# Scores' factors on another engine, with their operand in another memory, and a new plan, in a fused attention and two-MoE kernel

## The chip, the cores and the metric

One core of a Trainium2 chip runs the whole kernel. The metric is the device time in microseconds (us) of one execution. Engines, by the names that the profile uses: PE is TensorE (PEld its weight loads), DVE is VectorE, ACT is ScalarE, POOL is GpSimd, SP is SyncE, which issues the DMAs. Each engine takes its instructions in the order of the program.

## What is computed

A linear attention with decay, then two feed-forward layers on its output, all in float32 (the weights of both layers arrive as float64):

```python
# r, k, v: 4 x 8 x 768 x 48 (batch, head, time, channel); w, u: 8 x 48
for t in range(S):
    cur = einsum('bhd,bhe->bhde', u * k[t], v[t])
    y[t] = einsum('bhd,bhde->bhe', r[t], state + cur)
    state = w[..., None] * state + einsum('bhd,bhe->bhde', k[t], v[t])
x = y as 3072 x 384
h = maximum(maximum(x @ w1, x @ w2), x @ w3)   # 384 -> 768
x = h @ w_out                                  # 768 -> 384
g = x @ w_gate                                 # 384 -> 1536
out = (silu(g) * (x @ w_val)) @ w_out2         # 1536 -> 384
```

## The kernel before

Time is cut into six blocks of 128 steps (NB = 6), and with four batches (B = 4) this makes 24 units of attention; unit n is batch n % 4 of block n // 4. The products of the two layers take float32 in two halves: for each operand a high half and a low half, three matmuls for a product (`product`, lines 420 to 424).

**A unit** has these steps. `load_unit` (285) brings `qk` (112 x 1024, the transposed r and k) and `nat` (128 x 1152: k, v, r by time). `prep_scores` (302) multiplies each half of `qk` by powers of the decay `P`: the scores' factors. `prep_bonus` (306) makes two products for the bonus term, `prep_keys` (311) scales the keys by `PT`. `scores` (328) is 8 matmuls into two banks of PSUM; `bonus` sums rows (L318), `fill` writes a diagonal (L326, ScalarE), `select` (337) copies the masked scores over it (L338, two instructions). `apply` (344) makes y from the state (L355) and from the masked scores (L364). `evacuate` copies y out. `outer` (374) is 8 matmuls, the outer products of keys and values (L383); `decay` (388) scales the state and `update` (392) adds the outer products (L397), or copies them in block 0 (L395). Each pool of PSUM `ps_s` (tags s0, s1), `ps_y`, `ps_u` holds one bank a tag; `ps_m` has four banks in turn for everything else.

**A weight job** is a piece of 576 columns (384 for w_b) of float64 weights that VectorE and ScalarE turn into two halves: `scale` (ScalarE), `top` (L250, L252), `rest` (L258, L260), `power` (L265) on VectorE, `put_hi` and `to_float` on ScalarE, `put_lo` (L276) on GpSimd or VectorE. Jobs 0 to 11 make w_a (the first layer's three matrices, two jobs for each of its 6 tiles f), 12 to 17 w_b, the rest w_c. Three buffers hold raw weights.

**The stages.** After the set-up come the four units of block 0, then `branch` (589): all engines read a flag and skip a slow path (`recurrence`, not taken here). Block i of the first layer is then 18 products `m(i, f, j)` of 9 matmuls, with the units of block i + 1 between them, and the products `o`. After block 5 the second layer runs through its six blocks (g, silu, oo).

**What sets the order.** The code between lines 499 and 804 issues everything by hand. `order` (600 to 620) is TensorE's sequence, written out. For the other engines class `Plan` (88) keeps, for each step, the engines that may take it with a cost on each, what it needs, and a lag; `run` picks, again and again, the step that can start earliest by its own clock, weighted by what hangs on it, and emits it. So the costs in the table decide the order on VectorE, GpSimd, ScalarE and SyncE. In block 0 `scaled`, the factors, may go to VectorE or GpSimd (`both`), later to GpSimd alone (`one`). `warm` fills TensorE's planned idle time in block 0 with matmuls that nobody reads.

The lines that the change turns on:

```python
def prep_scores(n, q, eng):
    a = inp[n][0][:, q]
    eng.tensor_tensor(out=a, in0=a, in1=P[0:112], op=ALU.mult)
...
        p, tag = (ps_m, "m") if n < B else (ps_u, "u")
...
add(("scaled", n, q), both if first else one, [("load", n)],
```

Of the kernel before, what the change touches and what calls it, by code (L numbers as in the profile page):

```python
# [8 lines left out]
F32 = mybir.dt.float32  # L9
# [5 lines left out]
ALU = mybir.AluOpType  # L15
# [4 lines left out]
T = 128  # L20
# [7 lines left out]
FAR = 3  # L28
# [59 lines left out]
class Plan:  # L88
# [4 lines left out]
    def __init__(self, free, tensor_order):  # L93
        self.steps, self.free, self.tensor_order = {}, dict(free), tensor_order
        self.behind = {}

    def add(self, key, on, needs, do, lag=0.0, at=0.0, behind=None):


        if behind is not None:  # L100
            self.behind[key] = behind
        self.steps[key] = (on, list(needs), do, lag, at)

    def run(self, idle, hop=0.1):
# [22 lines left out]
        done, ready = {}, {}  # L127

# [8 lines left out]
        while ready:  # L137
# [28 lines left out]
def rwkv_moe(ctx: ExitStack, tc: tile.TileContext, qk, nat, kn, vn, rn, wcol, wh, uh, wup1, wout1, wup2, out):  # L166
# [332 lines left out]
    with tc.manual_schedule():  # L499
# [84 lines left out]
        def flag(_):  # L584
            nc.vector.tensor_reduce(out=off[:, NPAIR:], in_=spare[:, T:], axis=AX.X, op=ALU.max)
            nc.vector.tensor_scalar(out=slow_i, in0=off[:, NPAIR:], scalar1=1.0, scalar2=None, op0=ALU.min)
            nc.vector.tensor_copy(slow, slow_i)

        def branch(_):
            warm(8)  # L590
            general = nc.values_load(slow_i[0:1, 0:1], min_val=0, max_val=1)
            with tc.If(general != 0):
                recurrence(tc, kn, vn, rn, wh, uh, [xr[0]] + [x2[i] for i in range(1, FAR)] + y_far, h_tile)

# [49 lines left out]
        add = plan.add  # L644
        both, one = {"dve": 0.9, "pool": 1.4}, {"pool": 1.45}

# [7 lines left out]
        for k, (key, z, n, _) in enumerate(jobs):  # L654
            early = key[0] == "c" and key[1] < ASIDE
            own, pace, space = {}, [], []
            TOP, REST, POWER, share = (1.9, 1.8, 0.7, n / HALF) if key[0] != "c" else (2.2, 2.2, 0.9, 1.0) if early else (1.25, 1.25, 0.46, 1.0)
            if early:
# [6 lines left out]
            else:  # L665
# [8 lines left out]
            add(("float", k), cast, [("rest", k)], lambda e, k=k: to_float(k), **own)  # L674
            add(("lo", k), {"pool": 1.6 * share, "dve": 0.9 * share}, [("float", k), ("power", k), ("hi", k)],
                lambda e, k=k: put_lo(k, engine[e]), **own)
# [19 lines left out]
        for n in range(NB * B):  # L696
# [12 lines left out]
            add(("bonus", n), {"dve": 1.2, "pool": 2.15} if first else {"pool": 2.15}, [("arrived", n)],  # L709
                lambda e, n=n: prep_bonus(n, engine[e]))  # L710
            add(("keys", n), {"pool": 1.05}, [("bonus", n)], lambda e, n=n: prep_keys(n), at=9.6)
            pair = {2: 0, 4: 2}.get(n, n - 1 if n > 4 else None)
            add(("s", n), {"pe": 1.3}, [("scaled", n, 0), ("scaled", n, 1)] + bank_free["s", n]
                + ([("select", pair, 0), ("select", pair, 1)] if pair is not None else []), lambda e, n=n: scores(n))
            add(("a0", n), {"dve": 0.55}, [("bonus", n)] + ([("y", two)] if n > 1 else []), lambda e, n=n: bonus(n))
            for x in range(2):
# [6 lines left out]
                lambda e, n=n: evacuate(n))  # L723
            add(("u", n), {"pe": 0.02 if last else 0.6}, [("y", n), ("keys", n)] + bank_free["u", n]
                + ([("update", n - 1)] if n > B and n <= (NB - 1) * B else []), lambda e, n=n: outer(n))
            if first:
                add(("update", n), {"act": 0.55}, [("u", n)], lambda e, n=n: update(n))
            elif not last:
                add(("decay", n), {"pool": 0.62}, [("y", n)], lambda e, n=n: decay(n, engine[e]))
# [3 lines left out]
        add(("branch",), {"none": 0.0}, rows0 + [("flag",), ("u", B - 1)]  # L733
            + [("fill", n, x) for n in range(B) for x in range(2)], branch)
# [151 lines left out]
```

## Time and profile before

| | before |
|---|---|
| time, median of 3 runs | 882.13 us (881.97 to 882.39) |
| the profiled execution: its own time | 882.0 us |
| the profiled execution: its span | 880.3 us |
| TensorE busy | 855.5 us (97%) |
| VectorE busy | 437.9 us (50%) |
| ScalarE busy | 317.1 us (36%) |
| GpSimd busy | 242.4 us (28%) |
| chain that ended last | PE 87%, DVE 6%, issue 2% |

The span runs from the first to the last instruction of the profiled execution. The shares are means over the whole span, and the stages differ: VectorE is busy half of the time on average, but the page's slices show it at nine tenths in the first stages and at two tenths in the second layer. The granted clock of TensorE is a share of 2.4 GHz; it is at 0.5 in some stretches before 114 us and at 1.0 after that.

### The profile page before, as it was taken

What the parts mean: (1) busy time and instruction counts of PE and PEld (TensorE: products, weight loads), DVE (VectorE), ACT (ScalarE), POOL (GpSimd) and SP (SyncE); (2) the same over time, 40 slices, a digit from 0 to 9 for tenths busy, and PEclk for the clock granted to TensorE, in tenths of its full rate; (3) what the DMA queues carried; (4) which work ended last, traced back from release to release, by engine and by line L of the source; (5) the groups of instructions that cost most, each with busy time, mean ns of one, the idle gap of its engine ahead of it and who ended that gap; (6) DMA issues with size and microseconds to landing.
All of it is one profiled execution on the core that took longest, in us unless ns stands there. A gap on an engine that the chain in (4) does not pass through costs nothing.

```text
span 880.3 us, 11968 instructions
## 1 busy us (share of the span) xinstructions
PE 855.5 (97%) x4790; PEld 702.0 (80%) x4790; DVE 437.9 (50%) x610; ACT 317.1 (36%) x633; POOL 242.4 (28%) x207
## 2 busy tenths in 40 slices
PE   7888799999999999999999999999999999999998
PEld 6776588887887887888888888888888888888886
DVE  7899978765955954323469522222222222222212
ACT  4655654453453442222356421231122122123111
POOL 7386556454754753110123200010010000001000
PEclk9889999999999999999999999999999999999999
DMA  9545325534544543313034010000000000000001
GB/s 286 216 132 190 113 101 176 172 119 156 169 140 149 176 156 123 131 72 130 1 108 135 1 37 0 1 36 1 1 36 1 1 0 36 1 1 36 0 1 37
DMA packets 21723, 74.34 MB, mean 84 GB/s; under 512 B 2496, under 2 KB 3392, under 8 KB 20896
## 3 DMA queue, kind: packets, MB, share of 16 engines
q1 hardware_dynamic: 21664, 73.54, 25.2%
q8 instruction: 38, 0.62, 0.3%
q14 instruction: 21, 0.17, 0.1%
HBM read 58.39 MB, written 14.16 MB: 82 GB/s over the span
## 4 chain that ended last, share of the span: by engine, by line
PE 87%; DVE 6%; issue 2%; ACT 0%; DVEq 0%; ACTq 0%
PE g L423 11%; PE g L422 11%; PE g L424 11%; PE m L422 8%; PE m L424 7%; PE m L423 7%; PE oo L423 6%; PE oo L422 6%; PE oo L424 6%; PE o L422 3%; PE o L424 3%; PE o L423 3%; PE s L335 2%; PE y L364 2%; PE y L355 2%
## 5 line engine op out<-in xcount | busy, mean ns | idle before, releaser
L479 DVE TENSOR_TENSOR g<-mm,g 128x512 f32<-128x512 f32 x72 | 50.1, 696 | 242.1 <-PE g L424 242.1
L422 PE MATMUL g<-xhi,w_c 128*128 128x512 f32 x432 | 168.0, 389 | 0.0
L423 PE MATMUL g<-xlo,w_c 128*128 128x512 f32 x432 | 168.0, 389 | 0.0
L424 PE MATMUL g<-xhi,w_c 128*128 128x512 f32 x432 | 168.0, 389 | 0.0
L422 PE MATMUL m<-xhi,w_a 128*128 128x512 f32 x324 | 132.9, 410 | 1.1 <-DVE hs L456 1.1
L423 PE MATMUL m<-xlo,w_a 128*128 128x512 f32 x324 | 128.8, 398 | 1.9 <-POOL xlo L417 1.9
L424 PE MATMUL m<-xhi,w_a 128*128 128x512 f32 x324 | 128.3, 396 | 0.1
L417 POOL TENSOR_TENSOR xlo<-x,xhi 128x512 fp32r<-128x512 f32 x12 | 16.4, 1373 | 340.0 <-DVE g L479 281.8
L475 ACT ACTIVATE mm<-g 128x512 f32<-128x512 f32 x72 | 43.1, 599 | 152.5 <-PE g L424 152.4
L422 PEld LDWEIGHTS g<-xhi,w_c 128*128 128x128 f32 x432 | 81.1, 188 | 17.0
L424 PEld LDWEIGHTS g<-xhi,w_c 128*128 128x128 f32 x432 | 81.1, 188 | 16.8
L423 PEld LDWEIGHTS g<-xlo,w_c 128*128 128x128 f32 x432 | 81.1, 188 | 16.8
L484 ACT CAST gs<-g 128x512 fp32r<-128x512 f32 x72 | 42.3, 587 | 134.8 <-DVE g L479 134.8
L422 PE MATMUL oo<-gs,w_c 128*128 128x512 f32 x216 | 84.0, 389 | 0.0
L423 PE MATMUL oo<-gs,w_c 128*128 128x512 f32 x216 | 84.0, 389 | 0.0
L424 PE MATMUL oo<-gs,w_c 128*128 128x512 f32 x216 | 84.0, 389 | 0.0
L304 POOL TENSOR_TENSOR qk<-qk,P 112x512 f32<-112x512 f32 x45 | 67.2, 1499 | 41.4 <-DMA qk<-in_qk 41.4
L422 PEld LDWEIGHTS m<-xhi,w_a 128*128 128x128 f32 x324 | 62.2, 192 | 17.0 <-DVE hs L456 1.3
L424 PEld LDWEIGHTS m<-xhi,w_a 128*128 128x128 f32 x324 | 62.2, 192 | 14.2 <-POOL w_a L276 0.6
L423 PEld LDWEIGHTS m<-xlo,w_a 128*128 128x128 f32 x324 | 62.2, 192 | 14.1 <-POOL xlo L417 2.2
L456 DVE TENSOR_TENSOR gs<-g,gs 128x512 fp32r<-128x512 f32 x72 | 49.7, 690 | 40.9 <-ACT gs L484 40.9
L326 ACT ACTIVATE am<-aeye,a 128x128 f32<-128x128 f32 x192 | 59.2, 390 | 20.6 <-DVE a L318 20.6
(115 smaller groups left out, 1225.3 us busy)
## 6 DMA issues: line engine op xcount, KB each, us to landing
raw<-in_wup SPq DMA_DIRECT2D x36, 576.0 KB, 5.5
nat<-in_nat SPq DMA_DIRECT2D x22, 576.0 KB, 5.5
qk<-in_qk SPq DMA_DIRECT2D x24, 448.0 KB, 4.9
aside<-parts SPq DMA_DIRECT2D x12, 576.0 KB, 3.7
w_c<-aside SPq DMA_DIRECT2D x6, 1152.0 KB, 5.2
out<-ob SPq DMA_DIRECT2D x18, 256.0 KB, 2.1
y<-x SPq DMA_DIRECT2D x3, 768.0 KB, 10.7
raw<-in_wout SPq DMA_DIRECT2D x6, 384.0 KB, 4.5
```

The lines of the kernel that those rows point to most:

```text
L304: eng.tensor_tensor(out=a, in0=a, in1=P[0:112], op=ALU.mult)
L326: eng.mul(o, aeye, f)
L335: nc.tensor.matmul(sc[n][x][:, j], a[r:r + D, 1, j], a[r:r + D, 0, j], start=True, stop=True)
L355: nc.tensor.matmul(y[r:r + m, j], st[b][r:r + D, j * D:j * D + m], a[r:r + D, 0, j], start=j == 0, stop=False, skip_group_check=True)
L364: nc.tensor.matmul(y[r:r + m, j], v[:, h * D:h * D + m], am[:, x, j], start=not i, stop=True, skip_group_check=bool(i))
L422: nc.tensor.matmul(p, wh_, xh, start=first, stop=False)
L423: nc.tensor.matmul(p, wh_, xl, start=False, stop=False)
L424: nc.tensor.matmul(p, wl_, xh, start=False, stop=last)
L456: nc.vector.tensor_tensor(out=g[1], in0=p, in1=g[0].bitcast(F32), op=ALU.subtract)
L475: nc.scalar.activation(out=hs[i, f], in_=banks["g", i, f, 0], func=AF.Silu)
L479: nc.vector.tensor_tensor(out=p, in0=hs[i, f], in1=p, op=ALU.mult)
L484: nc.scalar.copy(t[:, 0], banks["g", i, f, 1])
```

## The change

Four things are changed. The new file is longer by 7 lines ahead of the helpers and by 29 at its end, so that L304 before is L311 after, L441 is L448 and L383 is L390.

1. From unit 4 on the factors (`scaled`) go to VectorE, and their second operand is a copy of `P` in PSUM (`late["P"]`, named `powers`), which ScalarE makes right after the branch in the bank of the pool `ps_u`.
2. That bank is no longer free for outer products, so from unit 4 on these are written into bank s0, where the unit's scores were. The scores of unit n + 1 therefore wait for the state update of unit n.
3. The outer products of block 0 leave the sequence ahead of the branch: those of units 0 and 1 come after `m(0, 0, 0)`, those of units 2 and 3 after `m(0, 1, 0)`. The slow path takes its scratch memory from elsewhere.
4. The plan has a port: steps on GpSimd, and the listed steps on VectorE (`SHARED`, without the factors from unit 4 on), start no earlier than the last of them ends. Its costs for these steps are lower than before.

```diff
+    SHARED = ("top", "rest", "power", "lo", "xlo", "ylo", "scaled", "bonus", "choose")
...
                     start, cost = max(t, free[e]), steps[k][0][e]
+                    if e == "pool" or e == "dve" and k[0] in self.SHARED and (k[0], k[1] > 3) != ("scaled", True):
+                        start = max(start, port)
...
             free[e] = start + cost
+            if e == "pool" or e == "dve" and k[0] in self.SHARED and (k[0], k[1] > 3) != ("scaled", True):
+                port = start + cost
...
-        eng.tensor_tensor(out=a, in0=a, in1=P[0:112], op=ALU.mult)
+        eng.tensor_tensor(out=a, in0=a, in1=late["P"] if n >= B else P[0:112], op=ALU.mult)
...
-            p, tag = (ps_m, "m") if n < B else (ps_u, "u")
+            p, tag = (ps_m, "m") if n < B else (ps_s, "s0")
...
+        def powers(_):
+            t = ps_u.tile([128, NPAIR, T], F32, tag="u", name="powers")
+            late["P"] = t[0:112]
+            nc.scalar.copy(late["P"], P[0:112])
...
-        order = [(q, n) for q, n in zip("ssyuyussyuyu", (0, 1, 0, 0, 1, 1, 2, 3, 2, 2, 3, 3))]
+        order = [(q, n) for q, n in zip("ssyyssyy", (0, 1, 0, 1, 2, 3, 2, 3))]
...
+                order += [("u", n) for n in range(B) if i == 0 and n // 2 == f]
...
-        both, one = {"dve": 0.9, "pool": 1.4}, {"pool": 1.45}
+        both, one = {"dve": 0.65, "pool": 1.07}, {"pool": 1.07}
...
-                add(("scaled", n, q), both if first else one, [("load", n)],
+                add(("scaled", n, q), both if first else {"dve": 0.69}, [("load", n)] + ([] if first else [("powers",)]),
...
-                + ([("select", pair, 0), ("select", pair, 1)] if pair is not None else []), lambda e, n=n: scores(n))
+                + ([("select", pair, 0), ("select", pair, 1)] if pair is not None else [])
+                + ([("update", n - 1)] if B < n <= (NB - 1) * B else []), lambda e, n=n: scores(n))
```

In the listings below, `a_0` to `a_3` are the row sums of the bonus of units 0 to 3, `am` a unit's masked scores, `r` and `kv` the r, k and v of units 2 and 3, `nat` those of the others, `t` and `raw` a weight job's tiles, `h` and `m` the products of the first layer.

VectorE ahead of the branch, where it prepares block 0; before:

```order
L318 TENSOR_REDUCE a_0_213<-nat_109 128x8
L304 TENSOR_TENSOR qk_113<-qk_113,P 112x512
L338 COPY_PREDICATED am_214<-mask,s_0_226 128x512
L338 COPY_PREDICATED am_214<-mask,s_0_227 128x512
L318 TENSOR_REDUCE a_1_260<-nat_114 128x8
L308 TENSOR_TENSOR r_106<-kv_118,r_106 128x384
L309 TENSOR_TENSOR r_106<-r_106,ub 128x384
L304 TENSOR_TENSOR qk_117<-qk_117,P 112x512
```

and after:

```order
L325 TENSOR_REDUCE a_0_227<-nat_109 128x8
L345 COPY_PREDICATED am_228<-mask,s_0_216 128x512
L345 COPY_PREDICATED am_228<-mask,s_0_217 128x512
L325 TENSOR_REDUCE a_1_267<-nat_114 128x8
L592 TENSOR_REDUCE off<-spare 128x1
L593 TENSOR_SCALAR slow_i<-off 128x1
L594 CAST slow<-slow_i 128x1
L345 COPY_PREDICATED am_268<-mask,s_1_249 128x512
L325 TENSOR_REDUCE a_2_302<-r_106 128x8
```

The bonus products of units 2 and 3 and the factors of units 1 and 2 have left VectorE's queue; both are on GpSimd now. VectorE keeps the factors of unit 0.

VectorE in block 0 behind the branch, at the second and third product of its first tile; before:

```order
L441 TENSOR_TENSOR m_0_2_725<-h_0_721,m_0_2_725 128x512
L265 TENSOR_SCALAR raw_676<-t_707 128x576
L250 TENSOR_SCALAR t_741<-t_741 128x576
L252 SCALAR_TENSOR_TENSOR t_741<-raw_704,t_741 128x576
L318 TENSOR_REDUCE a_4_806<-nat_670 128x8
L456 TENSOR_TENSOR hs_0_789<-m_0_2_725,hs_0_789 128x512
```

and after:

```order
L448 TENSOR_TENSOR m_0_2_695<-h_0_654,m_0_2_695 128x512
L311 TENSOR_TENSOR qk_668<-qk_668,powers 112x512 x2
L272 TENSOR_SCALAR raw_617<-t_642 128x576
L463 TENSOR_TENSOR hs_0_739<-m_0_2_695,hs_0_739 128x512
L325 TENSOR_REDUCE a_4_756<-nat_669 128x8
```

Unit 4's two factors stand on VectorE between a maximum and a conversion step. VectorE is one weight job less advanced at this place: it finishes job 3 here, and job 4 before.

GpSimd at the same place; before:

```order
L417 TENSOR_TENSOR xlo_664<-xr_309,xhi_663 128x512 x2
L304 TENSOR_TENSOR qk_669<-qk_669,P 112x512
L308 TENSOR_TENSOR nat_670<-nat_670 128x384
L309 TENSOR_TENSOR nat_670<-nat_670,ub 128x384
L304 TENSOR_TENSOR qk_669<-qk_669,P 112x512
L276 TENSOR_TENSOR w_a_680<-raw_661 128x576
L313 TENSOR_TENSOR nat_670<-nat_670,PT 128x384
```

and after:

```order
L424 TENSOR_TENSOR xlo_612<-xr_306,xhi_611 128x512 x3
L283 TENSOR_TENSOR w_a_422<-raw_131 128x576
L283 TENSOR_TENSOR w_a_686<-raw_133 128x576
L315 TENSOR_TENSOR nat_669<-nat_669 128x384
L316 TENSOR_TENSOR nat_669<-nat_669,ub 128x384
L283 TENSOR_TENSOR w_a_686<-raw_617 128x576
L283 TENSOR_TENSOR w_a_798<-raw_683 128x576
L320 TENSOR_TENSOR nat_669<-nat_669,PT 128x384
```

The factors are gone from GpSimd, and it has all three splits of the block's input and the w_a product of job 2, of which VectorE had one each.

## Rows read from the trace of the kernel before

**Rows 1.** The page, part 1: busy us, share of the span, instructions.

```profile
PE 855.5 (97%) x4790; PEld 702.0 (80%) x4790; DVE 437.9 (50%) x610; ACT 317.1 (36%) x633; POOL 242.4 (28%) x207
```

**Rows 2.** Windows behind the first stages: length, busy us of each engine, granted clock.

```profile
122.00:165.00 43.00, 43.00 (x333) 34.58 (x333) 31.78 (x55) 23.81 (x59) 20.00 (x20) 1.00 0.36 116
165.00:330.00 165.00, 165.00 (x1151) 134.25 (x1149) 113.18 (x139) 75.33 (x167) 95.47 (x76) 1.00 0.48 158
```

**Rows 3.** Window from branch to w_b: PE, PEld, DVE, ACT, POOL busy, granted clock.

```profile
37.19:113.70 76.51, 62.98 (x429) 48.97 (x427) 73.77 (x95) 43.09 (x90) 54.41 (x43) 0.89 0.54 169
```

**Rows 4.** TensorE's waits from 0 to 130 us: total, times, longest.

```profile
PE y L364 <- DVE am L338: 5.5, 6, 2.4
```

**Rows 5.** VectorE's groups from 37.2 to 113.7 us: busy us, mean ns, idle.

```profile
L252 DVE SCALAR_TENSOR_TENSOR t<-raw,t 128x576 uint32<-128x576 uint32 x9 | 12.3, 1367 | 0.3
...
L258 DVE TENSOR_SCALAR raw<-raw 128x576 uint32<-128x576 uint32 x10 | 7.1, 715 | 0.4 <-DVEq L592 0.2
...
L441 DVE TENSOR_TENSOR h<-h,m 128x512 f32<-128x512 f32 x5 | 3.4, 678 | 0.0
```

**Rows 6.** Timeline of VectorE where GpSimd is idle: start, us, engine, line.

```profile
50.45 0.76 DVE L252 SCALAR_TENSOR_TENSOR t<-raw,t 128x576 uint32<-128x576 uint32 x1
...
66.29 0.68 DVE L441 TENSOR_TENSOR h<-h,m 128x512 f32<-128x512 f32 x1
66.89 0.46 DVE L265 TENSOR_SCALAR raw<-t 128x576 uint32<-128x576 uint32 x1
```

**Rows 7.** GpSimd's groups from 37.2 to 113.7 us, columns as in rows 5.

```profile
L304 POOL TENSOR_TENSOR qk<-qk,P 112x512 f32<-112x512 f32 x10 | 15.6, 1565 | 3.5 <-DMA qk<-in_qk 3.5
L276 POOL TENSOR_TENSOR w_a<-raw 128x576 fp32r<-128x576 f32 x10 | 13.1, 1315 | 20.2 <-ACT raw L272 19.9 <-DVE t L250 0.4
...
L308 POOL TENSOR_TENSOR nat<-nat 128x384 f32<-128x384 f32 x5 | 6.3, 1264 | 0.0
```

**Rows 8.** Timeline of all engines from 0 to 44 us, around the branch.

```profile
10.23 1.78 POOL L304 TENSOR_TENSOR qk<-qk,P 112x512 f32<-112x512 f32 x1 [1.90 <-DMA qk<-in_qk]
...
11.99 1.00 POOL L308 TENSOR_TENSOR nat<-nat 128x384 f32<-128x384 f32 x1
...
15.26 1.15 DVE L308 TENSOR_TENSOR r<-kv,r 128x384 f32<-128x384 f32 x1 [0.60 <-DMA r<-in_nat]
...
22.01 2.45 ACT L326 ACTIVATE am<-aeye,a 128x128 f32<-128x128 f32 x8 [0.32 <-DVE a L318]
...
37.19 0.46 DVE L258 TENSOR_SCALAR raw<-raw 128x576 uint32<-128x576 uint32 x1 [0.22 <-DVEq L592]
...
38.57 1.64 ACT L413 CAST xhi<-xr 128x512 fp32r<-128x512 f32 x3
38.75 1.15 POOL L276 TENSOR_TENSOR w_a<-raw 128x576 fp32r<-128x576 f32 x1 [6.87 <-ACT raw L272]
```

**Rows 9.** Line 304 up to 40 us: shortest, median and longest in ns.

```profile
L304 POOL TENSOR_TENSOR qk<-qk,P x5: 1252/1582/1779, 6.6 to 18.7; 112x512 f32<-112x512 f32 x5
L304 DVE TENSOR_TENSOR qk<-qk,P x3: 693/1222/1746, 6.0 to 19.1; 112x512 f32<-112x512 f32 x3
```

**Rows 10.** Timelines at block 1's start, VectorE and TensorE.

```profile
113.62 1.94 DVE L408 COPY_PREDICATED xr<-slow,x 128x1536 f32<-128x1536 uint8 x1
...
121.65 0.39 PE L424 MATMUL o<-hs,w_b 128*128 128x512 f32 x1
121.88 0.39 PE L422 MATMUL m<-xhi,w_a 128*128 128x512 f32 x1
```

**Rows 11.** GpSimd's waits from 110 to 330 us: total, times, longest.

```profile
POOL qk L304 <- DMA qk<-in_qk: 16.3, 7, 4.4
```

**Rows 12.** The chain in order of time: a unit's scores, y and outer products.

```profile
128.16 1.09 PE s L335 x16
...
132.54 1.02 PE y L364 x15
133.55 0.45 PE u L383 x15
```

More of the change, by code (lines that the diff above doesn't have):

```diff
@@ L126, in run @@
                     stack.append(d)
-        done, ready = {}, {}
+        done, ready, port = {}, {}, 0.0
         def open_(k):
@@ L587, in flag, with scratch @@
             nc.vector.tensor_copy(slow, slow_i)
+        def scratch(shape, name):
+            if not room_:
+                room_.extend(x2_space(q, [128, NK * NT], f"rec_{q}") for q in (3, 4))
+            q, at = {"wu": (0, 0), "st": (0, 96), "kv": (0, 672), "cur": (1, 0), "kr": (1, 576), "vy": (1, 1344)}[name]
+            n = 1
+            for x in shape[1:]:
+                n *= x
+            t = room_[q][:, at:at + n]
+            names = "abc"[:len(shape) - 1]
+            return t.rearrange(f"p ({' '.join(names)}) -> p {' '.join(names)}", **dict(zip(names, shape[1:])))
+        room_ = []
+        def powers(_):
+            t = ps_u.tile([128, NPAIR, T], F32, tag="u", name="powers")
+            late["P"] = t[0:112]
+            nc.scalar.copy(late["P"], P[0:112])
         def branch(_):
@@ L592, in branch @@
             with tc.If(general != 0):
-                recurrence(tc, kn, vn, rn, wh, uh, [xr[0]] + [x2[i] for i in range(1, FAR)] + y_far, h_tile)
+                recurrence(tc, kn, vn, rn, wh, uh, [xr[0]] + [x2[i] for i in range(1, FAR)] + y_far, scratch)
         def attention_closed(_):
@@ L656, in rwkv_moe @@
             own, pace, space = {}, [], []
-            TOP, REST, POWER, share = (1.9, 1.8, 0.7, n / HALF) if key[0] != "c" else (2.2, 2.2, 0.9, 1.0) if early else (1.25, 1.25, 0.46, 1.0)
+            TOP, REST, POWER, share = (1.22, 1.22, 0.46, n / HALF) if key[0] != "c" else (1.22, 1.22, 0.46, 1.0) if early else (1.25, 1.25, 0.46, 1.0)
             if early:
@@ L674, in rwkv_moe @@
             add(("float", k), cast, [("rest", k)], lambda e, k=k: to_float(k), **own)
-            add(("lo", k), {"pool": 1.6 * share, "dve": 0.9 * share}, [("float", k), ("power", k), ("hi", k)],
+            add(("lo", k), {"pool": 1.2 * share, "dve": 0.76 * share}, [("float", k), ("power", k), ("hi", k)],
                 lambda e, k=k: put_lo(k, engine[e]), **own)
@@ L706, in rwkv_moe @@
             for q in range(2):
-                add(("scaled", n, q), both if first else one, [("load", n)],
+                add(("scaled", n, q), both if first else {"dve": 0.69}, [("load", n)] + ([] if first else [("powers",)]),
                     lambda e, n=n, q=q: prep_scores(n, q, engine[e]))
-            add(("bonus", n), {"dve": 1.2, "pool": 2.15} if first else {"pool": 2.15}, [("arrived", n)],
+            add(("bonus", n), {"dve": 1.1, "pool": 1.95} if first else {"pool": 1.95}, [("arrived", n)],
                 lambda e, n=n: prep_bonus(n, engine[e]))
-            add(("keys", n), {"pool": 1.05}, [("bonus", n)], lambda e, n=n: prep_keys(n), at=9.6)
+            add(("keys", n), {"pool": 0.97}, [("bonus", n)], lambda e, n=n: prep_keys(n), at=9.6)
             pair = {2: 0, 4: 2}.get(n, n - 1 if n > 4 else None)
             add(("s", n), {"pe": 1.3}, [("scaled", n, 0), ("scaled", n, 1)] + bank_free["s", n]
-                + ([("select", pair, 0), ("select", pair, 1)] if pair is not None else []), lambda e, n=n: scores(n))
+                + ([("select", pair, 0), ("select", pair, 1)] if pair is not None else [])
+                + ([("update", n - 1)] if B < n <= (NB - 1) * B else []), lambda e, n=n: scores(n))
             add(("a0", n), {"dve": 0.55}, [("bonus", n)] + ([("y", two)] if n > 1 else []), lambda e, n=n: bonus(n))
@@ L723, in rwkv_moe @@
                 lambda e, n=n: evacuate(n))
-            add(("u", n), {"pe": 0.02 if last else 0.6}, [("y", n), ("keys", n)] + bank_free["u", n]
-                + ([("update", n - 1)] if n > B and n <= (NB - 1) * B else []), lambda e, n=n: outer(n))
+            add(("u", n), {"pe": 0.02 if last else 0.6}, [("y", n), ("keys", n)] + ([("branch",)] if first else []) + bank_free["u", n]
+                , lambda e, n=n: outer(n))
             if first:
@@ L728, in rwkv_moe @@
             elif not last:
-                add(("decay", n), {"pool": 0.62}, [("y", n)], lambda e, n=n: decay(n, engine[e]))
+                add(("decay", n), {"pool": 0.54}, [("y", n)], lambda e, n=n: decay(n, engine[e]))
                 add(("update", n), {"dve": 0.37}, [("u", n), ("decay", n)], lambda e, n=n: update(n))
@@ L732, in rwkv_moe @@
         add(("flag",), {"dve": 0.5}, [("s", 1)], flag, lag=3.0)
-        add(("branch",), {"none": 0.0}, rows0 + [("flag",), ("u", B - 1)]
+        add(("powers",), {"act": 0.6}, [("branch",)], powers)
+        add(("branch",), {"none": 0.0}, rows0 + [("flag",)]
             + [("fill", n, x) for n in range(B) for x in range(2)], branch)
```

## The prediction

> **What bounds the kernel now.** I read the page first: TensorE is busy for 855.5 of 880.3 us [rows 1]. The windows then say where the rest lies. From 122 to 330 us TensorE is busy all the time at a granted clock of 1.00, with VectorE at 113 of the last 165 us and GpSimd at 95 [rows 2], so a faster VectorE is worth nothing there. From 37.2 to 113.7 us it is VectorE that is busy for 73.8 of 76.5 us and TensorE for 63.0, at a mean granted clock of 0.89, so partly at the lower of its two levels (1.2 of 2.4 GHz) [rows 3]. What TensorE waits for up to 130 us is above all VectorE's masked scores (L338) [rows 4]. This stretch begins where VectorE leaves the branch and ends with its last step on the third w_b tile. What lies before it is a chain too, and behind it TensorE runs on without a gap: its first product of block 1 starts at 121.88 [rows 10]. Every us by which that start comes earlier comes off the end, unless a new wait appears.
>
> Why VectorE is full shows in its groups of that stretch. The five steps that convert a weight job of 576 columns (L250, L252, L258, L260, L265; five groups from 12.3 down to 7.1 us) took 46.9 us in 48 instructions [rows 5]. Alone, the three scalar ones take 0.46 us and the two-tensor ones 0.76 [rows 6], which would be 27.8 in all, or 2.9 a job. So 19.1 us are lengthening, and 4.0 more if w_b's fifteen shorter ones are lengthened in the same proportion: 23.1. The instructions that take an operand from PSUM (L441) stand at 0.678, the same as alone [rows 5, 6]. GpSimd was busy for 54.4 us meanwhile [rows 3], so a microsecond of it cost VectorE 23.1/54.4 = 0.42. GpSimd pays too: a scores' factor averages 1.57 us here, where the shortest is 1.25 [rows 7, 9].
>
> **The change part by part.** The sum is made against the profiled execution's 882.0 us, which is its span and 1.7 around it, 0.1 under the median of 882.1.
>
> *Start to the branch.* VectorE loses the bonus products and factors of units 2 and 3; GpSimd gets them, and its four key products move behind. GpSimd then sets the pace. The factors' input of unit 1 lands at 10.2; two factors at 1.25 (the shortest, since VectorE now has little beside them) give 12.7; two bonus products at 1.00 give 14.7; unit 2's r has landed by 15.3, and two products give 17.3; four factors give 22.3; two bonus products 24.3 [rows 8, 9]. A row sum (by its columns under 0.6), eight fills (2.45) and a masked copy (0.7, by L441's columns) make 28.0. VectorE then converts job 0 (2.9) and starts job 1 (1.2): 32.1, and 0.2 for the branch give 32.3, where it was 37.2 [rows 8]. That is **4.9 saved**. With the factors at 1.58 [rows 9] it would be 34.3, with the fills' second half hidden 31.0. Block 0's outer products no longer stand ahead of the branch; VectorE was not waiting for them, so that is nothing here.
>
> *Branch to the last w_b step, 76.5 us before.* (a) Ten factors of 15.6 us leave GpSimd [rows 7]; at 0.42 that takes 6.6 off VectorE. (b) Eight factors come to VectorE with the powers in PSUM. The nearest row is L441, the same columns with one PSUM operand: 0.68, of which 0.08 lies under the next instruction (66.29 to 66.89 in [rows 6]), so 8 x 0.6 = 4.8 more. The other bound is 8 x 1.22 = 9.8, if they were lengthened like the three with SBUF operands alone [rows 9]. (c) VectorE enters one job less advanced (2.9) but hands a split (0.7) and a w_a product (1.65) to GpSimd: 0.6 more. Together 76.5 - 6.6 + 4.8 + 0.6 = 75.3. (d) The planner now books one port for GpSimd and for those VectorE steps, so that GpSimd may stand under the PSUM ones. The limit is the sum of what cannot overlap: VectorE's conversions 36.5 (12 and a half jobs, w_b's at two thirds), and GpSimd's 31.7 (11 w_a at 1.15 [rows 8], 2 w_b at two thirds, 3 splits at the factors' 1.25, 12 products of nat at 1.0, 3 decays at half of that), so 68.2. The same sum for the kernel before gives 80 where 76.5 was measured; it is a little too strict. I take the middle of 75.3 and 68.2: **71.8, 4.7 saved**. GpSimd already waits 20 us for ScalarE there [rows 7], and with the factors gone it has less of a backlog: an engine that is sometimes empty cannot stand under VectorE's other work at will.
>
> The Trainium skill ("SBUF — State Buffer", Who interferes with whom) says that a GpSimd instruction and a VectorE instruction with two SBUF inputs, or in a two-port mode, shut each other out for a whole instruction. By it 68.2 would be a hard floor; the trace agrees in kind, but not to the last tenth. Another rule of the skill speaks against this edit ("VectorE: DVE Perf Modes", Rules for kernel authors): what is read often should be copied from PSUM to SBUF first, and here an operand goes the other way. With the powers left in SBUF the eight factors would cost 9.8 instead of 4.8, by the 1.22 of [rows 9]; L441's 0.678 speaks for the change.
>
> *Hidden parts.* The copy of the powers is one ScalarE instruction, no dearer than the fills' 2.45; ScalarE is busy for 43 of 76.5 us [rows 3]. The four outer products (0.45 each [rows 12], 1.8) now stand between TensorE's first products, whose 18 x 9 matmuls at 0.23 [rows 10] with four units' attention need some 53 of the 71.8 us; without that cover they would cost 1.8. The loads of units 4 and 5 now wait for the first two of them, and VectorE reaches unit 4's factors some 14 us after the branch. From unit 4 on, outer products share a bank with the next unit's scores, so these wait for the state update; two products of TensorE, 4.1 us, lie between, against one short VectorE instruction. I put all four at nothing.
>
> *Handover.* Before, 8.2 us lay between VectorE's last w_b step and block 1's first product, and TensorE filled them. After, TensorE waits there for w_b's low half (0.8) and has 21 matmuls left (4.8): 5.6. VectorE has three evictions (2.0) and the choice L408 (1.9 [rows 10]); then ScalarE's split takes 0.55 and GpSimd's 1.25 each: 5.7 for the first, 8.2 for the third. The third goes into the last three matmuls of the first product, which so ends 8.9 after the step, instead of 8.2 + 2.0 = 10.2. **1.1 saved** with some loss for the third, between 0 and 2.
>
> Sum: 4.9 + 4.7 + 1.1 = 10.7, so 882.0 - 10.7 = **871.3**.
>
> **Rivals.** *The port is the only bound.* The stretch falls to its port sum of 68.2, or to 65.0 by the ratio 76.5/80. For it: two engines that were both full. Against it: GpSimd's waits for ScalarE [rows 7]. It gives 882.0 - 4.9 - 8.3 - 1.1 = 867.7 down to 864.5; I write 867.
>
> *VectorE takes the port's place: no change.* VectorE's own work rises by 5.4; if all 23.1 us of lengthening stayed, because GpSimd's remaining products are all met head on, the stretch would take 81.9, and 882.0 - 4.9 + 5.4 - 1.1 = 881.4. Against it: a third of GpSimd's time is gone.
>
> *VectorE's queue waits for loads: slower.* GpSimd waited for the factors' input seven times after 110 us, 16.3 us in all, 4.4 at most [rows 11]. On VectorE such a wait holds up the masked scores queued behind it. From the end of a unit's scores (129.25) to the part of y that needs them (132.54) TensorE has 3.3 us [rows 12], and two masked copies take 1.4: 1.9 of slack. The gain of 10.7 over 16 units is 0.67 each, so it decides from waits of 2.6 us in every unit; at 4.4 in half of the units it is 871.3 + 8 x 2.5 = 891.3. Against it: the planner places the factors behind a load's booked arrival, and VectorE has 52 idle us from 165 to 330 [rows 2].
>
> **How the numbers follow.** Forecast, 865 to 879: 0.62. Port alone: 0.15. VectorE in the port's place: 0.10, of which 0.07 falls within 0.2% of the time before (880.3 to 883.9, about what a measurement of this kernel can tell from no change) and 0.03 below. Loads on VectorE: 0.13, of which 0.02 falls in that band. So faster 0.80, same 0.09, slower 0.11. The range, 862 to 881, takes in the first two, with the start at 31.0 and the stretch at 65 as its lower end, and the third up to its middle; left out are the loads and the far tail.
>
> **What would show it.** VectorE's first step behind the branch should start near 32, its last w_b step end near 104, block 1's first product start near 110.5. The factors should stand at about 0.68 on VectorE, and L252's successor at some 1.15 us instead of 1.37. TensorE should still have no wait behind 125 us. The prediction is wrong if the factors are lengthened, if TensorE waits for scores or masked copies in blocks 1 to 4, or if GpSimd's start chain ends after 27 us.

## The result, and the profile after

The changed kernel took 872.66 us (median of 4 runs, 870.99 to 874.36), the kernel before 882.05 beside it (4 runs, 881.41 to 882.39): a ratio of 0.9898 with a 95% interval of 0.9887 to 0.991. That is 9.4 us less; 10.7 were forecast. The profiled execution took 872.5 us, with a span of 870.8; that of before took 882.0, so the two traces hold 9.5 us of difference.

Part 1 of the page of the changed kernel (busy us, share of the span, instructions; before in [rows 1]):

```profile
PE 851.7 (98%) x4794; PEld 696.3 (80%) x4794; DVE 400.1 (46%) x629; ACT 317.8 (36%) x634; POOL 193.8 (22%) x188
```

VectorE lost 37.8 us of busy time and GpSimd 48.6, and the kernel gained 9.5: most of this lies where TensorE is busy all the time anyway. The windows show it (length, busy us of PE, PEld, DVE, ACT, POOL, granted clock, DMA). The first goes from VectorE's first step behind the branch to its last step on the third w_b tile, and answers to [rows 3]; the other two answer to [rows 2].

```profile
32.28:105.17 72.89, 61.99 (x492) 47.52 (x491) 67.95 (x106) 45.15 (x96) 36.98 (x32) 0.95 0.61 184
122.00:165.00 43.00, 43.00 (x367) 34.99 (x367) 34.81 (x60) 20.53 (x43) 17.38 (x19) 1.00 0.51 167
165.00:330.00 165.00, 165.00 (x1134) 133.84 (x1134) 93.91 (x148) 72.54 (x163) 53.97 (x53) 1.00 0.46 151
```

From 165 to 330 us VectorE does 19.3 us less and GpSimd 41.5 us less than in [rows 2], and nothing comes of it. In the first stretch GpSimd is busy for 37.0 us instead of 54.4 and VectorE for 68.0 of 72.9 instead of 73.8 of 76.5.

The places that the prediction named, in the timelines of VectorE, GpSimd and TensorE (start, duration, engine, line; before in [rows 8] and [rows 10]):

```profile
22.71 0.99 POOL L316 TENSOR_TENSOR r<-r,ub 128x384 f32<-128x384 f32 x1
...
32.28 0.75 DVE L265 TENSOR_SCALAR raw<-raw 128x576 uint32<-128x576 uint32 x1 [0.58 <-DVEq L618]
...
104.81 0.36 DVE L272 TENSOR_SCALAR raw<-t 128x384 uint32<-128x384 uint32 x1
...
109.95 3.80 POOL L424 TENSOR_TENSOR xlo<-xr,xhi 128x512 fp32r<-128x512 f32 x3
...
110.88 0.39 PE L429 MATMUL m<-xhi,w_a 128*128 128x512 f32 x1
...
113.81 0.50 PE L430 MATMUL m<-xlo,w_a 128*128 128x512 f32 x1 [0.29 <-POOL xlo L424]
```

GpSimd's last bonus product ends at 23.7; VectorE leaves the branch at 32.28 instead of 37.19; its last w_b step ends at 105.17 instead of 113.70; block 1's first product starts at 110.88 instead of 121.88. It is stretched, because TensorE waits in it for each of GpSimd's three splits: its ninth matmul ends at 114.54, that of before at 124.08. So the 9.5 us are 4.9 up to the branch, 76.5 - 72.9 = 3.6 in the stretch, and 1.0 in the handover (10.4 from the last w_b step to that ninth matmul before, 9.4 after). Behind it the kernels take 756.2 and 756.3 us (880.3 - 124.08 and 870.8 - 114.54), so the whole gain lies ahead of it.

VectorE's groups in the stretch (busy us, mean ns, idle). [rows 5] has before's L252, L258 and L441, which are L259, L265 and L448 here; the other three conversion steps of before come first:

```profile
L260 DVE SCALAR_TENSOR_TENSOR raw<-raw 128x576 uint32<-128x576 uint32 x10 | 11.1, 1109 | 0.3
L250 DVE TENSOR_SCALAR t<-t 128x576 uint32<-128x576 uint32 x9 | 8.5, 942 | 0.0
L265 DVE TENSOR_SCALAR raw<-t 128x576 uint32<-128x576 uint32 x10 | 7.9, 789 | 0.1
```

And after:

```profile
L259 DVE SCALAR_TENSOR_TENSOR t<-raw,t 128x576 uint32<-128x576 uint32 x10 | 10.9, 1090 | 0.3
L267 DVE SCALAR_TENSOR_TENSOR raw<-raw 128x576 uint32<-128x576 uint32 x11 | 10.7, 973 | 0.4
L265 DVE TENSOR_SCALAR raw<-raw 128x576 uint32<-128x576 uint32 x11 | 8.1, 738 | 0.8 <-DVEq L618 0.6
L272 DVE TENSOR_SCALAR raw<-t 128x576 uint32<-128x576 uint32 x11 | 6.0, 547 | 0.2
L257 DVE TENSOR_SCALAR t<-t 128x576 uint32<-128x576 uint32 x10 | 5.6, 558 | 0.0
...
L311 DVE TENSOR_TENSOR qk<-qk,powers 112x512 f32<-112x512 f32 x8 | 5.1, 679 | 0.0
...
L448 DVE TENSOR_TENSOR h<-h,m 128x512 f32<-128x512 f32 x5 | 3.4, 675 | 0.0
```

The factors with the powers in PSUM take 0.679 us each, the 0.68 that L448 takes. L259 fell from 1.37 to 1.09. The five conversion steps together took 46.9 us in 48 instructions before and take 41.3 us in 53 now.

TensorE's waits from 24 to 130 us (total, times, longest; none is listed from 125 to 875 us):

```profile
PE m L430 <- POOL xlo L424: 2.9, 5, 1.1
PE m L429 <- ACT h L443: 2.8, 1, 2.8
PE m L431 <- POOL w_a L283: 2.3, 3, 1.2
...
PE s L342 <- DVE st L404: 1.6, 2, 1.1
```

The waits for masked scores of [rows 4] are gone. The last row stands in place of one of before, where it was the outer products that waited for the state update:

```profile
PE u L383 <- DVE st L397: 4.9, 3, 2.8
```

Now scores and outer products use one bank, and it is the next unit's scores that wait, for 1.6 us instead of 4.9.

### The profile page after: what moved, and what is told of

Same layout as the page of the kernel before. It is cut to its first block, busy times and chain, and to the rows that moved or that the text cites. A ratio compares the mean times of both kernels' runs of the same rounds, so it can differ in the third digit from the quotient of the medians.

```text
span 870.8 us, 11929 instructions
## 1 busy us (share of the span) xinstructions
PE 851.7 (98%) x4794; PEld 696.3 (80%) x4794; DVE 400.1 (46%) x629; ACT 317.8 (36%) x634; POOL 193.8 (22%) x188
## 4 chain that ended last, share of the span: by engine, by line
PE 88%; DVE 5%; issue 2%; POOL 1%; DMA 1%; ACT 1%; POOLq 0%; SPq 0%; DVEq 0%; ACTq 0%
PE g L431 11%; PE g L429 11%; PE g L430 11%; PE m L429 8%; PE m L430 7%; PE m L431 7%; PE oo L431 6%; PE oo L429 6%; PE oo L430 6%; PE o L429 3%; PE o L430 3%; PE o L431 3%; PE s L342 2%; PE y L371 2%; PE y L362 2%
## 5 line engine op out<-in xcount | busy, mean ns | idle before, releaser
L424 POOL TENSOR_TENSOR xlo<-x,xhi 128x512 fp32r<-128x512 f32 x18 | 23.5, 1332 | 329.8 <-ACT xhi L420 329.8
L448 DVE TENSOR_TENSOR h<-h,m 128x512 f32<-128x512 f32 x36 | 24.7, 685 | 79.7 <-PE m L431 61.1
```

The costliest lines, as they stand in the source:

```text
L424: eng.tensor_tensor(out=lo[:, k], in0=t[:, k], in1=hi[:, k].bitcast(F32), op=ALU.subtract)
L448: nc.vector.tensor_tensor(out=hs[i, f] if j == 1 else p, in0=hs[i, f], in1=p, op=ALU.max)
```

## The experiments

The parts were undone one at a time (e1 to e4), the factors were left out of either kernel (e5, e6), the plan was put into the kernel before (e7), and e8 to e11 carry the finding on. Times are medians. "Branch" is the start of VectorE's first step behind the branch, "w_b" the end of its last step on the third w_b tile, both in the profiled execution. A trace is one run: those of e1 and e9 are the fastest of their kernels, those of e3 and e11 the slowest, so the last column compares only roughly. In every trace but e7's, what follows the ninth matmul of block 1 takes 756.2 to 756.4 us.

| kernel | time, us | before beside it | ratio, 95% interval | branch, w_b |
|---|---|---|---|---|
| before | 882.05 | | 1 | 37.2, 113.7 |
| after | 872.66 | 882.05 | 0.9898, 0.9887 to 0.991 | 32.3, 105.2 |
| e1 powers from SBUF | 878.31 | 881.54 | 0.9965, 0.9949 to 0.9981 | 33.1, 107.0 |
| e2 no port in the plan | 880.56 | 881.54 | 0.9994, 0.9979 to 1.0009 | 36.6, 111.9 |
| e3 factors on GpSimd | 881.31 | 881.54 | 0.9998, 0.9986 to 1.0009 | 34.3, 116.2 |
| e4 outer products early | 872.39 | 881.54 | 0.989, 0.9873 to 0.9906 | 35.2, 104.6 |
| e5 before, no factors | 875.23 | 881.85 | 0.9923, 0.9906 to 0.994 | 37.0, 106.8 |
| e6 after, no factors | 871.63 | 881.85 | 0.9885, 0.9868 to 0.9901 | 33.2, 104.2 |
| e7 before, new plan | 882.17 | 881.85 | 1.0006, 0.9992 to 1.002 | 35.0, 111.8 |
| e8 early powers | 871.27 | 881.85 | 0.9878, 0.9862 to 0.9895 | 35.9, 104.5 |
| e9 and true landings | 868.30 | 881.97 | 0.986, 0.9836 to 0.9883 | 30.9, 100.3 |
| e10 after, true landings | 871.77 | 882.61 | 0.9884, 0.9868 to 0.9901 | 33.4, 104.5 |
| e11 splits on VectorE | 869.05 | 882.61 | 0.9846, 0.9827 to 0.9866 | 32.9, 102.3 |

**e1: the powers from SBUF.** Order and plan stay as they are; only the second operand of the factors changes.

```diff
-        eng.tensor_tensor(out=a, in0=a, in1=late["P"] if n >= B else P[0:112], op=ALU.mult)
+        eng.tensor_tensor(out=a, in0=a, in1=P[0:112], op=ALU.mult)
```

> Order and plan of the changed kernel, but VectorE's factors from unit 4 on read the powers from SBUF instead of PSUM. Theory A (what counts is that a VectorE instruction with two SBUF operands and a GpSimd instruction shut each other out): the factors stand at 0.9 to 1.2 us on average instead of 0.65 to 0.69, GpSimd's products beside them get longer too, VectorE's last w_b step ends 3 to 4 us later than 105.2, and the time is 875 to 877 us. Rival B (the gain is only that the factors left GpSimd's queue; where the operand lies does not matter): factors at 0.69, time 872 to 873.5.

5.6 us of the 9.4 went, somewhat more than expected. Its runs lie further apart than those of the others (875.57 to 880.5 in 7), and the profiled one is its fastest, so its trace shows only the smaller part of the loss. It shows the mechanism all the same. First VectorE's factors, in pairs, then GpSimd beside them:

```profile
46.79 1.28 DVE L311 TENSOR_TENSOR qk<-qk,P 112x512 f32<-112x512 f32 x2
57.90 2.72 DVE L311 TENSOR_TENSOR qk<-qk,P 112x512 f32<-112x512 f32 x2
74.06 3.52 DVE L311 TENSOR_TENSOR qk<-qk,P 112x512 f32<-112x512 f32 x2
87.61 2.55 DVE L311 TENSOR_TENSOR qk<-qk,P 112x512 f32<-112x512 f32 x2
```

```profile
48.58 1.15 POOL L283 TENSOR_TENSOR w_a<-raw 128x576 fp32r<-128x576 f32 x1 [2.93 <-DVE raw L272]
...
73.41 1.75 POOL L283 TENSOR_TENSOR w_a<-raw 128x576 fp32r<-128x576 f32 x1 [3.92 <-DVE t L257]
75.11 0.95 POOL L397 TENSOR_TENSOR st<-st,pw 112x192 f32<-112x192 f32 x1
76.03 1.01 POOL L320 TENSOR_TENSOR nat<-nat,PT 128x384 f32<-128x384 f32 x1
```

The pair at 46.79 has GpSimd idle beside it and takes 1.28 us, as from PSUM. The pair at 74.06 stands beside three instructions of GpSimd and takes 3.52. The operand in SBUF costs nothing by itself; it costs the meeting with GpSimd. With the port in the plan but not the operand in PSUM, 3.2 us of the gain are left against the kernel before beside it (881.54 - 878.31).

**e2: no port in the plan.** The new costs stay.

```diff
-                    if e == "pool" or e == "dve" and k[0] in self.SHARED and (k[0], k[1] > 3) != ("scaled", True):
-                        start = max(start, port)
```

> The changed kernel with the port left out of the planner, its new costs kept. Theory A (the planner's knowledge of the port places GpSimd's work under VectorE's other work, my term (d) of 3.3 us, and with it part of the 4.9 us at the start): 875 to 880 us, VectorE's first step behind the branch later than 33, more lengthening per microsecond of GpSimd than in the changed kernel. Rival C (the lower costs and the moved factors do it; the port in the plan is idle): within 1.5 us of 872.7.

Nearly the whole gain is gone, although the factors still run on VectorE from PSUM. Where the plan put them tells a part of why. Here are the changed kernel's factors in the stretch, with GpSimd's instructions at those times:

```profile
60.52 1.28 DVE L311 TENSOR_TENSOR qk<-qk,powers 112x512 f32<-112x512 f32 x2
75.00 1.28 DVE L311 TENSOR_TENSOR qk<-qk,powers 112x512 f32<-112x512 f32 x2
87.05 1.28 DVE L311 TENSOR_TENSOR qk<-qk,powers 112x512 f32<-112x512 f32 x2
```

```profile
60.14 1.15 POOL L283 TENSOR_TENSOR w_a<-raw 128x576 fp32r<-128x576 f32 x1 [2.75 <-issue]
61.25 1.01 POOL L315 TENSOR_TENSOR nat<-nat 128x384 f32<-128x384 f32 x1
...
74.36 1.74 POOL L283 TENSOR_TENSOR w_a<-raw 128x576 fp32r<-128x576 f32 x1 [2.04 <-DVE t L257]
...
86.40 1.75 POOL L283 TENSOR_TENSOR w_a<-raw 128x576 fp32r<-128x576 f32 x1 [2.56 <-DVE t L257]
```

And the same two engines in e2, where L309 is the factors' line:

```profile
53.96 1.27 DVE L309 TENSOR_TENSOR qk<-qk,powers 112x512 f32<-112x512 f32 x2
66.35 1.28 DVE L309 TENSOR_TENSOR qk<-qk,powers 112x512 f32<-112x512 f32 x2
79.76 1.28 DVE L309 TENSOR_TENSOR qk<-qk,powers 112x512 f32<-112x512 f32 x2
```

```profile
54.88 1.59 POOL L313 TENSOR_TENSOR nat<-nat 128x384 f32<-128x384 f32 x1 [1.46 <-DMA nat<-in_nat]
...
68.40 1.15 POOL L281 TENSOR_TENSOR w_a<-raw 128x576 fp32r<-128x576 f32 x1 [4.60 <-issue]
...
81.81 1.15 POOL L281 TENSOR_TENSOR w_a<-raw 128x576 fp32r<-128x576 f32 x1 [3.67 <-ACT h L441]
```

With the port booked, three of the four pairs stand under GpSimd's work (4.1 of the eight factors' 5.4 us, counted from the two timelines). Without it all four pairs stand wholly or mostly in GpSimd's idle time (1.5 of the nine factors' 6.1 us are under its work), and GpSimd's products then meet the conversions: a microsecond of GpSimd lengthens these by 0.37 us in e2, by 0.31 in the changed kernel and by 0.43 in the kernel before (their time in the stretch less the durations alone, w_b's steps taken at 0.35 and 0.56 us). So in this stretch the port in the plan and the powers in PSUM work together: PSUM makes the factors able to stand under GpSimd, the port makes the planner put them there. That is not all of e2's loss. Of the 6.8 us by which its last w_b step is later, 4.3 are there at the branch, ahead of any factor from PSUM; how much of that the plan's order there cost was not tried.

**e3: the factors on GpSimd**, with the powers in SBUF; port, costs and shared bank stay.

```diff
...
-                add(("scaled", n, q), both if first else {"dve": 0.69}, [("load", n)] + ([] if first else [("powers",)]),
+                add(("scaled", n, q), both if first else one, [("load", n)],
...
```

> The changed kernel with the factors from unit 4 on back on GpSimd, powers in SBUF, outer products still in the scores' bank, the planner with its port. Theory A: the start stays near 32.3, the stretch up to w_b takes 77 instead of 72 to 73 us, time 877 to 879 us. Rival C (the new plan alone makes the gain): 872 to 874. Rival D (the factors make it all, also what I put down to the start): 881 to 883.

No gain at all, 2 us above what the sum of terms said and inside rival D's range. The rest of the change brings nothing while GpSimd holds the factors.

**e4: block 0's outer products back ahead of the branch**, where they stood before.

```diff
-        order = [(q, n) for q, n in zip("ssyyssyy", (0, 1, 0, 1, 2, 3, 2, 3))]
+        order = [(q, n) for q, n in zip("ssyuyussyuyu", (0, 1, 0, 0, 1, 1, 2, 3, 2, 2, 3, 3))]
...
```

> The changed kernel with block 0's outer products back ahead of the branch, in TensorE's sequence of the kernel before. Theory A (VectorE and GpSimd set the start; these 0.6 us each lie beside them): 872 to 874.5 us, VectorE's first step behind the branch at 32.3 to 33.5. Rival E (the move of the outer products is what brings the branch forward): the branch comes 2 to 5 us later and the time is 875 to 878.

The time is that of the changed kernel, as forecast. But the branch, expected at 32.3 to 33.5, came 2.9 us later than in it, and the stretch behind was 3.4 shorter (69.5). VectorE had done two more steps of job 1 ahead of the branch, which took 0.75 and 1.71 us behind it in the changed kernel:

```profile
33.83 0.76 DVE L267 SCALAR_TENSOR_TENSOR raw<-raw 128x576 uint32<-128x576 uint32 x1
35.15 0.98 DVE L272 TENSOR_SCALAR raw<-t 128x576 uint32<-128x576 uint32 x1 [0.56 <-DVEq L618]
```

So when the branch comes says little of the end. The conversions before and behind it are one queue, and its sum counts.

**e5 and e6: no factors for units 4 to 19**, in the kernel before and in the changed one. Both leave that scaling out and nothing else.

```diff
     def prep_scores(n, q, eng):
+        if n >= B:
+            return
```

> The kernel before (882), leaving out the scaling of the scores' inputs by the powers for units 4 to 19; nothing else is changed, so its output is not the reference's there. Ten factors (15.6 us) go from GpSimd between the branch and the last w_b step. Theory A (a microsecond of GpSimd costs VectorE 0.42): the stretch of 76.5 falls by 6.6 to about 70, the time to 874 to 876. Theory B (the shared port is the only bound, so the factors stood in it with all their 15.6 us of which some 12 were not under anything else): 870 to 872. Theory D (before's plan is bound by other things than the factors): 879 to 882.

> The changed kernel (872.7), leaving out the same scaling for units 4 to 19, so that its output is not the reference's there. Eight factors of 0.6 to 0.68 go from VectorE's queue in the stretch. Theory A: VectorE is the bound for about half of that stretch, so 2.4 to 4.9 us less: 868 to 870.5. Theory B (the port is the bound, the factors on PSUM lie beside GpSimd's work): within 1 us of 872.7, 871.5 to 873.5.

The windows of the stretch, of e5 and then of e6 (columns as above):

```profile
36.95:106.81 69.86, 60.84 (x427) 47.24 (x425) 66.90 (x95) 42.35 (x90) 39.00 (x33) 0.90 0.57 180
```

```profile
33.19:104.18 70.99, 62.00 (x491) 47.34 (x491) 64.01 (x98) 45.00 (x96) 37.89 (x31) 0.95 0.60 188
```

On GpSimd the factors cost 881.85 - 875.23 = 6.6 us, and e5's stretch is 69.9 where 76.5 - 6.6 was forecast. On VectorE, under the port, they cost 872.66 - 871.63 = 1.0 us; the two intervals overlap, so this may be nothing, and cannot be 4.8. Between e5 and e6 lie 3.6 us that belong to the rest of the change.

**e7: the kernel before with the port and the new costs alone.**

> The kernel before with the planner's port and the new costs alone; factors stay on GpSimd with the powers in SBUF, outer products ahead of the branch and in their own bank. By what the changed kernel with its factors on GpSimd showed (881.3), the port in the plan has nothing to work with while the factors use the port themselves: 879.5 to 883. Rival: booking the port is worth what the forecast's middle gave it, some 3.5 us, by itself: 877 to 879.5.

No gain, like e3. Its third w_b step ended 1.9 us earlier than before's, and the ninth matmul of block 1 3.0 earlier; yet TensorE then waited 1.7 us for masked scores in block 1, where before it has no wait, and took 758.3 us from there to the end.

**e8: block 0's factors from PSUM too.** The powers are copied ahead of the first factors, and all eight run on VectorE.

```diff
...
+        early_P = ps_m.tile([128, NPAIR, T], F32, tag="m", name="powers_0")[0:112]
+        nc.scalar.copy(early_P, P[0:112])
...
-                add(("scaled", n, q), both if first else {"dve": 0.69}, [("load", n)] + ([] if first else [("powers",)]),
+                add(("scaled", n, q), {"dve": 0.69}, [("load", n)] + ([] if first else [("powers",)]),
```

> The changed kernel (872.7), with the powers copied to PSUM before the first factors, so that block 0's eight factors too run on VectorE from PSUM: 7.5 us of factors leave GpSimd and 2.8 us of factors leave the SBUF port ahead of the branch. Theory A' (what counts is the sum of the work on the shared port from the start, not when the branch falls): VectorE's first step behind the branch moves from 32.3 to 27 to 30, and most of that reaches the end: 867 to 870.5. Rival (the loads set the start: unit 3 and the first weights land only then, or VectorE's queue waits for GpSimd's products of units 2 and 3): 871.5 to 874.

1.4 us less than after, with overlapping intervals. The branch came at 35.9, not before 30. ScalarE's timeline in e8 shows why:

```profile
22.81 0.75 ACT L224 ACTIVATE t<-raw 128x576 f32<-128x576 f32 x1 [2.67 <-DMA raw<-in_wup]
23.46 2.43 ACT L333 ACTIVATE am<-aeye,a 128x128 f32<-128x128 f32 x8
```

ScalarE stands 2.7 us before L224 for the first weight job, with unit 2's fills queued behind it, and VectorE's masked copies wait for those. The planner believed that job landed at 17.5 us.

**e9: the true landings** in e8's plan: units 1 to 3 and the first three weight jobs are booked close to where e8's trace has them.

```diff
-                add(("fetch", k), {"none": 0.0}, [], lambda e: None, at=17.5 + 1.7 * k)
+                add(("fetch", k), {"none": 0.0}, [], lambda e: None, at=22.8 + 1.5 * k)
...
-        arrive = ((5.5, 7.3), (9.0, 10.6), (11.9, 13.5), (14.8, 16.4))
+        arrive = ((5.5, 7.3), (9.6, 13.1), (14.2, 17.7), (17.8, 21.4))
```

> The kernel with block 0's factors from PSUM too (871.3), with the landings that the planner books in block 0 put where the trace of that kernel shows them (unit 3's r at 21.4 instead of 16.4, the first weight job at 22.8 instead of 17.5). In that kernel ScalarE stood 2.7 us for the first weight job with unit 2's fills queued behind it, VectorE 1.5 and 2.0 us for ScalarE, and VectorE left the branch at 35.9. Theory A' (the start is lost in the order that wrong landings gave): VectorE's first step behind the branch at 29.5 to 32, the last w_b step 2 to 4 us earlier than 104.5, the time 867 to 869.5. Rival (the stretch behind the branch is set by TensorE's own work and by x's split, so that an earlier branch is given back): 870.5 to 872.5.

868.30 us is the lowest of the medians, and its interval lies just below that of the changed kernel (0.9883 against 0.9887). It overlaps with e8's, though no run of e9 (867.58 to 870.4) took as long as any of e8 (870.49 to 871.98). The same place on ScalarE in e9, then VectorE behind the branch and TensorE's first product of block 1:

```profile
22.43 2.45 ACT L333 ACTIVATE am<-aeye,a 128x128 f32<-128x128 f32 x8 [0.98 <-DVE a L325]
24.79 0.72 ACT L224 ACTIVATE t<-raw 128x576 f32<-128x576 f32 x1
...
30.87 1.30 DVE L265 TENSOR_SCALAR raw<-raw 128x576 uint32<-128x576 uint32 x1
...
106.90 0.39 PE L429 MATMUL m<-xhi,w_a 128*128 128x512 f32 x1
```

The fills no longer stand behind the load, and everything up to block 1 comes 4.0 us earlier than in the changed kernel (106.90 against 110.88), in a trace of its fastest run. Against e8's trace not all is the order: 1.3 us are there already when unit 1's first factor starts, which waits for its load (9.97 against 11.28).

**e10: the true landings in the changed kernel alone**, with e9's second diff and not e8's.

> The changed kernel (872.7) with the booked landings of block 0 corrected alone, block 0's factors as they are (GpSimd and VectorE, powers in SBUF). If the corrected order is what made 871.3 into 868.3, it should make 872.7 into 869 to 870.5 here too. If the landings only matter once GpSimd no longer has the factors of block 0 (it is full until 27.5 us in the changed kernel, with or without them), 871.5 to 874.

871.77 is not told apart from after, and in the range expected if GpSimd's chain sets the start. That the landings matter only once the factors have left GpSimd fits e8 to e10, but it rests on the 3.0 us between e8 and e9.

**e11: block 0's three splits of x on VectorE**, in e9.

```diff
-                add(("xlo", i, k), both, [("xhi", i, k)], lambda e, i=i, k=k: split_lo((1, i), xr[i], k, engine[e]))
+                add(("xlo", i, k), both if i else {"dve": 0.76}, [("xhi", i, k)], lambda e, i=i, k=k: split_lo((1, i), xr[i], k, engine[e]))
```

> The kernel at 868.3 (factors of block 0 from PSUM, true landings) with block 0's three splits of x on VectorE instead of GpSimd. There they took 4.7 us on GpSimd, while VectorE's instructions with SBUF operands beside them took 1.3 to 1.7 instead of 0.46 to 0.76; on VectorE they should take 2.3. Theory A' (the sum of work on the shared port from the start to the last w_b step sets the end): 1.5 to 2.4 us less, 866 to 867. Rival (the first weight job's low half becomes late, so that TensorE starts later and the gain is given back): 867.8 to 869.5.

Not told apart from e9: the median is 0.75 us higher, the ratio lower (0.9846 against 0.986). The three splits took 1.89 us on VectorE where GpSimd took 4.68, yet in the traces the branch comes at 32.9 and the last w_b step ends 2.0 us later than in e9. These are the slowest run of the one and the fastest of the other, and 1.25 us of it lie in the landing of unit 1's load, ahead of every split (its first factor starts at 11.22 against 9.97). So whether the splits saved anything is open.

## Why the prediction held, and which of its terms did not

The sign, the size and the mechanism held: 872.7 was measured against 871.3, within the likeliest case, and the signs that it named are there, the last w_b step 1.2 us later than the 104 it gave. Its terms fared unequally. The letters are the prediction's; "stretch" is that from the branch to the last w_b step.

| term | forecast | measured | from |
|---|---|---|---|
| start to the branch | -4.9 | -4.9 | traces of before and after |
| (a) ten factors leave GpSimd | -6.6 | -6.6 | e5 against before |
| (b) eight factors on VectorE | +4.8 | +1.0 | e6 against after: what leaving them out gives back |
| the stretch in all, (a) to (d) | -4.7 | -3.6 | traces |
| handover | -1.1 | -1.0 | traces |
| all but the factors: start, (c), handover | -5.4, or -8.9 with (d) | -3.6 | e6 against e5 |

The start was right step by step: the last bonus product of GpSimd ended at 23.7 (24.3 forecast), VectorE's second step on job 1 at 31.7, the branch came at 32.3. The rate of 0.42 us of VectorE for a microsecond of GpSimd, taken from before's groups, gave e5's stretch to a tenth. The handover was right in its form too: TensorE reached its product 5.7 us after the last w_b step (5.6 forecast) and lost time on the splits; the sum had this for the third alone.

In VectorE's own account of the stretch, read from its groups in the two traces, the other terms come out near their sizes too. The factors add 5.1 us of busy time, where (b) had 4.8. One more job (2.9), less the split (0.7) and the w_a product (1.65) that GpSimd took, is the 0.6 of (c). The conversions, by far the largest part, are lengthened less: the five groups took 46.9 and 41.3 us, where the durations alone make 27.8 and 30.7, so 19.1 became 10.6; and w_b's fifteen shorter steps went from 11.1 to 7.6. That is 12.0 less, while VectorE's idle time rose from 2.7 to 4.9: together 9.8 less, where (a) and (d) had 10.1. Smaller steps make up the rest, half a microsecond.

What did not hold is that these terms are separate. The prediction charged (b) at its full 4.8 us and gave (d), the port, a price of its own, as a middle between two bounds. e1, e2 and e6 show that the two belong together. With the port in the plan, leaving the factors out gives back only 1.0, and VectorE is then idle for 7.0 of 71.0 us; undoing the operand in PSUM costs 5.6 of the end (e1), undoing the port 7.9, a part of it ahead of the branch (e2). As one term (b) and (d) were forecast at 4.8 - 3.5 = 1.3, near that 1.0. That the middle between 75.3 and 68.2 came so near is luck: the mechanism of (d) was right ("GpSimd may stand under the PSUM ones"), but no row gave its size.

The start and (c) are not separate either. The branch falls within one queue of conversions, and with the branch 2.9 us later e4 ends at the same time. Between e5 and e6, which both lack the factors, the branch comes 3.8 us earlier, the stretch is 1.1 us longer (69.9 to 71.0), where (c) had 0.6, and the handover is 1.3 shorter.

Of the parts put at nothing, the outer products' place was nothing (e4), and no wait for loads appeared on VectorE from 105 to 330 us, so the rival that ended slower did not come. The bank that scores now share made TensorE wait 1.6 us for the state update up to 130 us, less than the 4.9 that the outer products had waited for it before; what this brought or cost at the end was not measured by itself. The rival "The port is the only bound, 867" did not come, since the stretch took 72.9 us and not 68.2. The rival "VectorE takes the port's place, 881.4" is near what the kernel becomes without the port in the plan (e2, 880.6); with the port and the powers in SBUF it stands between (e1, 878.3).

The Trainium skill ("SBUF — State Buffer", Who interferes with whom) says that a VectorE instruction with two SBUF inputs contends with a GpSimd instruction that reads SBUF, and that one with at most one SBUF input, outside the two-port modes, does not. The traces agree: a pair of factors from SBUF was lengthened to as much as 3.52 us beside GpSimd in e1's stretch, one from PSUM took 1.27 or 1.28 in that of the changed kernel, beside GpSimd or not. The rule of the Trainium skill that the prediction set against the edit ("VectorE: DVE Perf Modes", Rules for kernel authors) is about elementwise work on the output of matmuls: accept the rate of a PSUM source, or copy to SBUF first if many operations follow. The powers are no output of a matmul, and reading them from PSUM was the faster choice here, by the 5.6 us of e1.

## What to carry to other kernels

Where two engines contend for a port, an instruction's price is not its duration but what it meets: give it an operand that keeps it off the port, and book the port in the plan so that it lands under the other engine's work. Both gained 9.4 us here, the port in the plan without the operand in PSUM 3.2 (e1), the operand without the port 1.0, which is within the noise (e2). Terms on both sides of a barrier through which one queue runs are one term: add up the queue's work up to the place where the bound changes, not the time at which the barrier falls. After a change that frees an engine at the start, try the planner's landing times where the trace has them: the medians fell by 3.0 us in e9, with intervals that overlap, and by 0.9, which is within the noise, while the engine was still full (e10).

## What the runs showed of the hardware

A pair of factors with both operands in SBUF takes 1.28 us where GpSimd is idle (e1), exactly as with one operand in PSUM; beside GpSimd it took 2.55 to 3.52 in e1's stretch. The load that unit 1's first factor waits for ended that wait between 10.0 and 11.3 us from one trace to the next, which is as much as some of the differences looked for here.

What TensorE's granted clock did to the times was not separated. In the 22 runs of the kernel before beside e1 to e4, the seven at a mean granted clock of 0.992 or more took 879.5 to 881.6 us (median 880.5), the other fifteen 880.7 to 883.0 (median 881.9), and the four runs of the changed kernel had 0.992 to 0.995. So some 1.5 of the 9.4 us may go with the clock; whether it shortens a run or is itself kept up by shorter waits, no run shows. One stretch shows no effect: from 50 to 70 us the clock was 0.87 in the changed kernel, so partly at the lower of its two levels, and 1.00 in e4, and their times agree within 0.3 us. The windows of either (columns as above), the changed kernel first:

```profile
50.00:70.00 20.00, 18.85 (x130) 14.82 (x129) 17.15 (x29) 12.39 (x30) 9.05 (x9) 0.87 0.50 144
```

```profile
50.00:70.00 20.00, 17.43 (x129) 12.64 (x127) 19.62 (x29) 13.42 (x31) 12.89 (x12) 1.00 0.49 146
```
